# Decode attention beside a SwiGLU feed-forward: how w_down, the end of V and the end of wo are loaded

## The chip, the cores and the metric

The kernel runs on one core of one Trainium2 chip. The metric is the device time of one execution in microseconds (us). One execution was also recorded by the hardware profiler; its trace gives the start and duration of every instruction and of every DMA packet. Engines: PE (matmuls; PEld its weight loads), DVE (vector), ACT (scalar), POOL (GpSimd), SP (here the issuer of nearly all DMAs). Sixteen DMA engines move the data of the core.

## The reference

One token is decoded by an attention block over a long cache and by a feed-forward block, and a scalar gate mixes the two. H is 32 heads, Sk 65,536 cached positions, Dh 128, D 512, F 1,792, all in bfloat16.

```
g = sigmoid((x * gate_w).sum(-1))
q = (x @ wq) in 32 heads of 128
p = softmax(q @ k_cache^T * 128**-0.5)         # 32 x 65536
a = (p @ v_cache) as 4096 values @ wo          # wo: 4096 x 512
b = (silu(x @ w_gate) * (x @ w_up)) @ w_down   # w_down: 1792 x 512
out = g * a + (1 - g) * b                      # 512 values
```

K and V have 536.9 MB each and are read once; everything else together is some 15 MB.

## The kernel before

**Tiles.** Each head's K and V are cut into G = 4 tiles of 16,384 positions; a tile is 128 partitions x 128 positions x 128 values, 4 MB, and n = 4h + g numbers the tiles from 0 to N - 1 = 127. All K and V tiles, and for a while wq, gate and up, w_down and the last wo rows, live in five slots of 4 MB. take(name) hands out the slot that has been free the longest and give(name) returns one, so the order of takes and gives in the program settles which load waits for which reader.

**Queues.** The schedule is written by hand: each engine runs its instructions in program order. SP issues the loads in program order; a load waits in SP until the readers of its slot are done, and the loads behind it wait with it. ACT issues only xT and gwT, at the start. Each DMA reports its completion through one of eight semaphores in turn, and a DMA is issued only when the last user of its semaphore has landed.

**A K tile.** DVE multiplies by the head's query (L254) and folds the 128 products to 64 or 32 by additions (L258); PE sums the rest with identity matmuls into S_ps (scores, L267); DVE folds it (L281). Per head, row_max and exponentials give P_sb, the weights.

**A V tile.** PE multiplies 4 columns of P_sb with 4 positions of the tile at a time: 32 matmuls of 128 x 512 into O_ps (values, L322). After a head's fourth V tile, ACT copies O_ps to O_sb (L335), head_turn turns it into a column by small matmuls (oh_ps, L351), ACT scales it to oT (L358), and project multiplies it with the head's 128 rows of wo into the two halves of a_ps (L365). For the last V tile the last TURNED = 8 positions are left to head_turn (L343).

**The loop.** A step loads and works one K tile and one V tile, with the V tiles some steps behind. load_wo(g) loads the wo rows of four heads (512 KB, two buffers) at v = 16g + 2, for g from 0 to 3. At v = N - 1 load_late loads the rows of the last 16 heads into a slot, in pieces of 5, 5, 4 and 2 heads. Heads 0 to 15 are projected in the loop, heads 16 to 31 after the last head_turn. The third and second to last V tiles come in two pieces each, the last one in pieces that end at columns 32, 64, 96, 112, 120 and 128.

**The start-up.** K 0 to 2 and wq are loaded first, then gate, K 3 and up. W_down (wd_t) takes the slot of K tile 1 behind scores(1). It lies on 64 partitions with 28 rows of w_down each, and comes in eight DMAs of 8 partitions (firsts lists the first of each, the step is 4), six ahead of load_k(4) and two behind it. load_k(4) takes the slot of wq, which is free once all queries are made. feed_forward_out runs in the step of K tile 4: two identity matmuls and an ACT copy bring the hidden values hT from 128 partitions x 14 to 64 x 28, then 28 matmuls of 64 x 512 make b_ps (L233), ACT copies it (L236) and four matmuls start a_ps with it (L238). The slot of w_down then goes to K tile 6 by the order of the free list.

Of the kernel before, what the change touches and what calls it, by code (L numbers as in the profile page):

```python
# [8 lines left out]
ACT = mybir.ActivationFunctionType  # L9
ALU = mybir.AluOpType  # L10
AXIS = mybir.AxisListType
P = 128
# [3 lines left out]
NB = 128  # L16
# [7 lines left out]
SPREAD = 40  # L24

WG = 4
LATE = 16
LATE_CUTS = (0, 5, 10, 14, LATE)
TURNED = 8
V_CUTS = {3: (0, 64, NB), 2: (0, 64, NB), 1: (0, 32, 64, 96, 112, NB - TURNED, NB)}  # L30


@with_exitstack
def kernel(
# [14 lines left out]
    nc = tc.nc  # L49
    bf16 = mybir.dt.bfloat16  # L50
    f32 = mybir.dt.float32

    _, H, Sk, Dh = A_k_cache.shape
    D = A_x.shape[2]
    F = B_w_gate.shape[1]
    KT = D // P
    FT = F // P
    G = Sk // (NB * P)
# [6 lines left out]
    consts = ctx.enter_context(tc.tile_pool(name="consts", bufs=1))  # L65
# [7 lines left out]
    psum_m = ctx.enter_context(tc.tile_pool(name="psum_m", bufs=2, space=bass.MemoryType.PSUM))  # L73
# [7 lines left out]
    def take(name):  # L81
        slot = free.pop(0)
        held[name] = slot
        return ring.tile(
            [P, NB * Dh], bf16, name=name.split(".")[0], tag=f"slot{slot}"
        )

    def give(name):
        free.append(held.pop(name))
# [14 lines left out]
    def load(dst, cache, n, name, cuts=(0, NB), slot=None):  # L104
        h, g = divmod(n, G)
        t = take(f"{name}.{n}") if slot is None else slot
        view = t.rearrange("p (j d) -> p j d", d=Dh)
        src = cache[0, h, g * NB * P : (g + 1) * NB * P, :].rearrange("(p j) d -> p j d", j=NB)
        for a, b in zip(cuts[:-1], cuts[1:]):
            nc.sync.dma_start(out=view[:, a:b, :], in_=src[:, a:b, :])  # L110
        dst[n] = view

    def load_k(n):
        load(K_tiles, A_k_cache, n, "K_t")

    def load_v(n):
        load(V_tiles, A_v_cache, n, "V_t", V_CUTS.get(N - n, (0, NB)))

# [9 lines left out]
    ident_b = consts.tile([P, P], bf16, name="ident_b")  # L128
# [29 lines left out]
    wo_tiles = {}  # L158

    def load_wo(g):  # L160
        wo_tiles[g] = wo_pool.tile([P, WG, D], bf16, name="wo_sb", tag="wo_sb")
        rows = A_wo[g * WG * P : (g + 1) * WG * P, :]
        nc.sync.dma_start(out=wo_tiles[g], in_=rows.rearrange("(h p) n -> p h n", p=P))

    def load_late(cuts):
        late = take("wo_late.0")[:, : LATE * D].rearrange("p (h n) -> p h n", n=D)
        rows = A_wo[(H - LATE) * P :, :].rearrange("(h p) n -> p h n", p=P)
        for a, b in zip(cuts[:-1], cuts[1:]):
            nc.sync.dma_start(out=late[:, a:b, :], in_=rows[:, a:b, :])
        return late  # L170

    def feed_forward_in():
        gu_ps = psum_m.tile([P, 2 * FT], f32, name="gu_ps", tag="misc")
        for w in range(2):
            cols = wgu_sb[:, w].rearrange("p t (m c) -> p t c m", c=FT)
            for ft in range(FT):
                for t in range(KT):
                    nc.tensor.matmul(
                        gu_ps[:, w * FT + ft : w * FT + ft + 1],
                        lhsT=cols[:, t, ft, :],  # L180
                        rhs=xT[:, t : t + 1],
                        start=(t == 0),
                        stop=(t == KT - 1),
                    )
        gu_sb = consts.tile([P, 2 * FT], f32, name="gu_sb")
        nc.scalar.activation(out=gu_sb, in_=gu_ps, func=ACT.Copy)
        eg = consts.tile([P, FT], f32, name="eg")
        nc.scalar.activation(out=eg, in_=gu_sb[:, :FT], func=ACT.Exp, scale=-1.0)
        return gu_sb, eg
# [32 lines left out]

    def feed_forward_out(hT, rest):
        b_ps = psum_m.tile([1, D], f32, name="b_ps", tag="misc")
        h_ps = psum_m.tile([HP, GT], f32, name="h_ps", tag="misc")
        for r in range(2):
            nc.tensor.matmul(
                h_ps[:, r * FT : (r + 1) * FT], lhsT=ident_b[:, r::2], rhs=hT, start=True, stop=True
            )
        h2 = consts.tile([HP, GT], bf16, name="h2")  # L230
        nc.scalar.activation(out=h2, in_=h_ps, func=ACT.Copy)  # L231
        for t in range(GT):
            nc.tensor.matmul(  # L233
                b_ps, lhsT=h2[:, t : t + 1], rhs=wd_sb[:, t, :], start=(t == 0), stop=(t == GT - 1)
            )
        nc.scalar.activation(out=b_sb, in_=b_ps, func=ACT.Copy, scale=rest)  # L236
        for i, a in enumerate(a_ps):
            nc.tensor.matmul(  # L238
                a, lhsT=ones_f[0:1, 0:1], rhs=b_sb[:, i * HD : (i + 1) * HD], start=True, stop=False
            )  # L240
# [22 lines left out]
    def scores(n):  # L263
        S = F_tiles[n] = psum_s.tile([P, NB, QUAD], f32, name="S_ps")
        width = width_of(n)
        for c in range(0, width, QUAD):
            nc.tensor.matmul(  # L267
                S,
                lhsT=ident_b,
                rhs=K_tiles[n][:, :, c : c + QUAD],  # L270
                start=(c == 0),
                stop=(c == width - QUAD),
            )
        del K_tiles[n]
        give(f"K_t.{n}")
# [84 lines left out]
        )  # L360

    def project(h):
        rows = wo_tiles[h // WG][:, h % WG, :] if h < H - LATE else wo_late[:, h - (H - LATE), :]
        for i, a in enumerate(a_ps):
            nc.tensor.matmul(  # L365
                a,
                lhsT=oT[:, h : h + 1],
                rhs=rows[:, i * HD : (i + 1) * HD],
                start=False,
                stop=(h == H - 1),  # L370
            )


    def score_tile(n):
        for _ in products(n):
            pass
        if n:
            fold(n - 1)
# [11 lines left out]
    score_tile(1)  # L390
    xs = gate_sum()
    scores(1)
    wd_t = take("wd_t.0")
    HP = P // 2
    GT = F // HP
    wd_sb = wd_t[:HP, : GT * D].rearrange("p (t n) -> p t n", t=GT)
    wd_rows = B_w_down.rearrange("(p t) n -> p t n", t=GT)
    firsts = (0, 1, 2, 3, 32, 33, 34, 35)

    def load_wd(i):  # L400
        part = slice(firsts[i], firsts[i] + 29, 4)
        nc.sync.dma_start(out=wd_sb[part], in_=wd_rows[part])

    for i in range(6):
        load_wd(i)
    for g in range(1, H // QG):
        queries(g)
    give("wq_t.0")
    eg2 = gate_exp(xs)
    load_k(4)  # L410
    load_wd(6)
    load_wd(7)
    score_tile(2)
    rest = gate_value(eg2)
    scores(2)
# [7 lines left out]
    v = 0  # L423
# [5 lines left out]
        steps.append((None, v))  # L429
        v += 1  # L430

    done = tot_ps = wo_late = None
    for n, v in steps:
        if n is not None and n > G:
            load_k(n)
        if v is not None:
            if v % (WG * G) == 2 and v // (WG * G) < (H - LATE) // WG:
                load_wo(v // (WG * G))
            if v:
                load_v(v)  # L440
            if v == N - 1:
                wo_late = load_late(LATE_CUTS)
        vector = iter(()) if n is None else products(n)
        top_of = None
        if n is None:
            top_of = H - 1 if F_tiles else None
        elif n % G == 0:
            top_of = n // G - 1
            vector = (i for a in (0, NB // 2) for i in products(n, a, a + NB // 2))
        if top_of is not None:  # L450
            next(vector, None)
            fold(top_of * G + G - 1)
            mT_ps = row_max(top_of)
            next(vector, None)
            exponentials(top_of, mT_ps)
        if n == G:
            hT = feed_forward_mid(*ff)
        for _ in vector:
            pass
        if n is not None and n % G:  # L460
            fold(n - 1)
        if tot_ps is not None:
            weight(*tot_ps)
            tot_ps = None
        if n == G:
            feed_forward_out(hT, rest)
            give("wd_t.0")
        if done is not None:
            head_turn(done, head_copy(done))
        if v is not None:  # L470
            values(v)
        if top_of is not None:
            tot_ps = top_of, total(top_of)
        if n is not None:
            scores(n)
        if done is not None and done < H - LATE:
            project(done)
        done = v // G if v is not None and v % G == G - 1 else None
    head_turn(H - 1, head_copy(H - 1))
    for h in range(H - LATE, H):  # L480
        project(h)

    out_sb = consts.tile([1, D], bf16, name="out_sb")
# [33 lines left out]
```

## Time and profile before

| What | Value |
|---|---|
| Median of 3 runs | 2534.09 us (2533.99 to 2534.16) |
| Profiled execution | 2534.41 us, of which the span of its instructions is 2532.6 us |
| DMA traffic | 1088.49 MB, mean 430 GB/s over the span |
| DVE busy | 2083.7 us (82%) |
| PE busy | 1533.7 us (61%), mean granted clock 0.772 |
| ACT busy | 77.7 us (3%) |
| K tile, issue to landing | 35.3 us (median) |
| V tile, issue to landing | 28.0 us (median) |

The profile names a group of instructions by engine, line and tiles (out<-in). A line of a timeline has start, duration, engine, line and operation, the number of instructions, and in brackets the engine's idle time before it with what ended that idle time. The chain of waits has start, duration and what it was; it runs back from the last instruction to whatever released each step. A table of windows has, for each stretch, its length, the busy time of PE, PEld, DVE, ACT and POOL with the number of instructions, the granted clock of PE, the mean busy share of the 16 DMA engines, and GB/s. A line of waits has who waited, for whom, the time in total, how often, and the longest one.

### The profile page before, as it was taken

To read this page: it belongs to the slowest core of one execution; us is meant where nothing else is said; L and a number is where in the kernel's file an instruction comes from. 1 tells how busy PE (TensorE), PEld (TensorE's weight loads), DVE (VectorE), ACT (ScalarE), POOL (GpSimd) and SP (SyncE) were. 2 spreads that over 40 slices of the span, in tenths; PEclk is the share of its full clock that TensorE was granted. 3 is DMA by queue.
4 is the path that set the end of the run, shared out by engine and by line. 5 is a ranking of instruction groups with operands and counts; after the bars stand their busy time and mean duration, and the time that the engine had idled before them with its cause. 6 is when DMAs were issued, how large, how long until landed. Compare 5 with 4: busy or idle time off the path is not lost.

```text
span 2532.6 us, 13195 instructions
## 1 busy us (share of the span) xinstructions
PE 1533.7 (61%) x5786; PEld 581.6 (23%) x5786; DVE 2083.7 (82%) x744; ACT 77.7 (3%) x208; POOL 0.9 (0%) x7
## 2 busy tenths in 40 slices
PE   4656656665566555555665566556656665665569
PEld 1222222222222112222222122222222221222223
DVE  7788888888887999988888888888888888888860
ACT  1000000000000000000000000000000000000000
POOL 0000000000000000000000000000000000000000
PEclk9777777777777787787777777777777777777779
DMA  9999999999999999999999999999999999999998
GB/s 412 418 431 433 435 432 430 434 433 432 431 433 434 431 433 434 432 431 434 433 432 433 434 432 432 435 431 432 432 434 432 431 435 433 431 434 433 432 432 351
DMA packets 43915, 1088.49 MB, mean 430 GB/s; under 512 B 4753, under 2 KB 9362, under 8 KB 10258
## 3 DMA queue, kind: packets, MB, share of 16 engines
q1 hardware_dynamic: 43570, 1087.65, 99.7%
q8 instruction: 45, 0.74, 0.1%
q14 instruction: 12, 0.10, 0.0%
q10 hardware_dynamic: 288, 0.00, 0.0%
HBM read 1087.64 MB, written 0.00 MB: 429 GB/s over the span
## 4 chain that ended last, share of the span: by engine, by line
DMA 71%; PE 23%; DVE 4%; issue 1%; ACT 0%; SPq 0%; DVEq 0%
DMA V_t<-in_A_v_cache_dram 63%; PE O_ps L322 21%; DMA K_t<-in_A_k_cache_dram 8%; DVE K_t L254 3%; DVE K_t L258 1%; PE S_ps L267 1%; DMA wo_late<-in_A_wo_dram 0%; PE b_ps L233 0%; DVE S_sb L281 0%; DVE m L287 0%; PE oh_ps L351 0%; PE a_ps L238 0%; ACT P_sb L300 0%; PE a_ps L365 0%; PE mT_ps L291 0%
## 5 line engine op out<-in xcount | busy, mean ns | idle before, releaser
L322 PE MATMUL O_ps<-V_t,P_sb 128*4 128x512 bf16 x4094 | 1154.5, 452 | 663.5 <-DMA V_t<-in_A_v_cache_dram 663.5
L254 DVE TENSOR_TENSOR K_t<-K_t,q_bc 128x16384 bf16<-128x16384 bf16 (+1 forms) x159 | 1117.2, 7026 | 357.9 <-DMA K_t<-in_A_k_cache_dram 346.7
L258 DVE TENSOR_TENSOR K_t<-K_t 128x8192 bf16<-128x8192 bf16 (+1 forms) x314 | 859.7, 2738 | 8.6
L322 PEld LDWEIGHTS <-P_sb 128*4 128x4 bf16 x4094 | 393.0, 97 | 1405.1 <-issue 1064.1
L267 PE MATMUL S_ps<-K_t,ident_b 128*128 128x512 bf16 x1056 | 263.3, 393 | 100.6 <-DVE K_t L258 100.6
L267 PEld LDWEIGHTS <-ident_b 128*128 128x128 bf16 x1056 | 98.0, 101 | 248.0 <-issue 158.0
L291 PE MATMUL mT_ps<-diag,ones_f 128*128 128x128 f32 x64 | 24.5, 483 | 150.1 <-ACT diag L289 150.1
L351 PE MATMUL oh_ps<-ident_f,O_sb 4*128 4x1 f32 x256 | 55.5, 334 | 74.5 <-ACT O_sb L335 74.5
L281 DVE TENSOR_REDUCE S_sb<-S_ps 128x128 f32<-128x512 f32 x128 | 87.5, 683 | 4.9 <-PE S_ps L267 4.9
L289 ACT ACTIVATE diag<-ident_f,m 128x128 f32<-128x128 f32 x32 | 12.8, 401 | 2118.7 <-DVE m L287 2118.7
L351 PEld LDWEIGHTS oh_ps<-ident_f,O_sb 4*128 4x128 f32 x256 | 52.8, 301 | 84.1 <-ACT O_sb L335 82.9
L291 PEld LDWEIGHTS mT_ps<-diag,ones_f 128*128 128x128 f32 x64 | 15.2, 295 | 166.7 <-ACT diag L289 166.7
L484 DVE CAST out_sb<-a_ps 1x256 bf16<-1x256 f32 x1 | 0.4, 412 | 56.6 <-PE a_ps L365 56.6
L300 ACT ACTIVATE P_sb<-S_sb,bias 128x512 bf16<-128x512 f32 x32 | 23.1, 722 | 1.0
L287 DVE TENSOR_REDUCE m<-S_sb 128x1 f32<-128x512 f32 x32 | 22.0, 686 | 1.1
L335 ACT ACTIVATE O_sb<-O_ps 4x512 f32<-4x512 f32 x32 | 18.3, 572 | 129.2 <-PE O_ps L322 129.2
L313 DVE RECIPROCAL recip<-tot_ps 128x1 f32<-128x1 f32 x32 | 5.1, 158 | 13.0 <-PE tot_ps L308 13.0
L308 PEld LDWEIGHTS tot_ps<-rowsum,ones_f 128*128 128x128 f32 x64 | 9.5, 188 | 14.0 <-issue 14.0
L233 PE MATMUL b_ps<-wd_t,h 64*1 64x512 bf16 x28 | 12.1, 625 | 0.3 <-ACT h L231 0.3
L308 PE MATMUL tot_ps<-rowsum,ones_f 128*128 128x1 f32 x64 | 12.2, 260 | 0.0
L358 ACT ACTIVATE oT<-oh_ps,rg 128x1 bf16<-128x1 f32 x32 | 8.4, 263 | 65.0 <-PE oh_ps L351 65.0
L296 DVE TENSOR_REDUCE top<-mT_ps 128x1 f32<-128x128 f32 x32 | 9.1, 284 | 1.0 <-PE mT_ps L291 1.0
(47 smaller groups left out, 75.2 us busy)
## 6 DMA issues: line engine op xcount, KB each, us to landing
K_t<-in_A_k_cache_dram SPq DMA_DIRECT2D x128, 4096.0 KB, 35.3
V_t<-in_A_v_cache_dram SPq DMA_DIRECT2D x125, 4096.0 KB, 28.0
V_t<-in_A_v_cache_dram SPq DMA_DIRECT2D x4, 2048.0 KB, 31.1
wq_t<-in_A_wq_dram SPq DMA_DIRECT2D x1, 3584.0 KB
V_t<-in_A_v_cache_dram SPq DMA_DIRECT2D x3, 1024.0 KB
wo_sb<-in_A_wo_dram SPq DMA_DIRECT2D x4, 512.0 KB, 38.8
gu_t<-in_B_w_gate_dram SPq DMA_DIRECT2D x1, 1792.0 KB
gu_t<-in_B_w_up_dram SPq DMA_DIRECT2D x1, 1792.0 KB
```

Of the source, the lines that this page charges most:

```text
L254: yield nc.vector.tensor_tensor(out=K, in0=K, in1=q_rep, op=ALU.mult)
L258: yield nc.vector.tensor_tensor(out=K[:, :, 0:half], in0=K[:, :, 0:half], in1=K[:, :, half : 2 * half], op=ALU.add,)
L267: nc.tensor.matmul(S, lhsT=ident_b, rhs=K_tiles[n][:, :, c : c + QUAD], start=(c == 0), stop=(c == width - QUAD),)
L281: nc.vector.tensor_reduce(out=S_tiles[h][:, g * NB : (g + 1) * NB], in_=F_tiles.pop(n), axis=AXIS.X, op=ALU.add)
L287: nc.vector.tensor_reduce(out=m, in_=S_tiles[h], axis=AXIS.X, op=ALU.max)
L289: nc.scalar.activation(out=diag, in_=ident_f, func=ACT.Copy, scale=m)
L291: nc.tensor.matmul(mT_ps, lhsT=ones_f, rhs=diag, start=True, stop=True)
L300: nc.scalar.activation(out=P_tiles[h], in_=S_tiles[h], func=ACT.Exp, bias=bias, scale=scale, accum_out=rowsum[:, h : h + 1],)
L308: nc.tensor.matmul(tot_ps, lhsT=ones_f, rhs=rowsum[:, h : h + 1], start=True, stop=True)
L322: nc.tensor.matmul(O_tiles[h], lhsT=P_tiles[h][:, g * NB + j : g * NB + j + 4], rhs=V_tiles[n][:, j : j + 4, :], start=(g == 0 and j == 0) ...
L335: nc.scalar.activation(out=O_sb, in_=O_tiles.pop(h), func=ACT.Copy)
L351: nc.tensor.matmul(oh_ps, lhsT=O_sb[:, c * Dh : (c + 1) * Dh], rhs=ident_f[0:4, c : c + 1], start=(c == 0 and not turned), stop=(c == 3),)
```

## The change

W_down lies on all 128 partitions with 14 rows each, and is one DMA of 1,792 KB. The Activation engine issues it, behind the queries' copies and the gate's exponential in its program; it takes the slot that wq gave back. K tile 4 is loaded ahead of it in the program and takes the slot of K tile 1. feed_forward_out multiplies hT directly: 14 matmuls of 128 x 512 take the place of the two identity matmuls, the ACT copy and 28 matmuls. The wo rows of all heads are loaded four heads at a time into the two wo buffers, the last four heads' rows behind the last V tile, and only heads 28 to 31 are projected after the last head_turn. The pieces of the last V tile that ended at columns 112 and 120 become one.

```diff
-LATE = 16
-LATE_CUTS = (0, 5, 10, 14, LATE)
 TURNED = 8
-V_CUTS = {3: (0, 64, NB), 2: (0, 64, NB), 1: (0, 32, 64, 96, 112, NB - TURNED, NB)}
+V_CUTS = {3: (0, 64, NB), 2: (0, 64, NB), 1: (0, 32, 64, 96, NB - TURNED, NB)}
...
-    def load_late(cuts):
-        late = take("wo_late.0")[:, : LATE * D].rearrange("p (h n) -> p h n", n=D)
-        rows = A_wo[(H - LATE) * P :, :].rearrange("(h p) n -> p h n", p=P)
-        for a, b in zip(cuts[:-1], cuts[1:]):
-            nc.sync.dma_start(out=late[:, a:b, :], in_=rows[:, a:b, :])
-        return late
...
         b_ps = psum_m.tile([1, D], f32, name="b_ps", tag="misc")
-        h_ps = psum_m.tile([HP, GT], f32, name="h_ps", tag="misc")
-        for r in range(2):
-            nc.tensor.matmul(
-                h_ps[:, r * FT : (r + 1) * FT], lhsT=ident_b[:, r::2], rhs=hT, start=True, stop=True
-            )
-        h2 = consts.tile([HP, GT], bf16, name="h2")
-        nc.scalar.activation(out=h2, in_=h_ps, func=ACT.Copy)
-        for t in range(GT):
-            nc.tensor.matmul(
-                b_ps, lhsT=h2[:, t : t + 1], rhs=wd_sb[:, t, :], start=(t == 0), stop=(t == GT - 1)
+        for t in range(FT):
+            nc.tensor.matmul(
+                b_ps, lhsT=hT[:, t : t + 1], rhs=wd_sb[:, t, :], start=(t == 0), stop=(t == FT - 1)
             )
...
-        rows = wo_tiles[h // WG][:, h % WG, :] if h < H - LATE else wo_late[:, h - (H - LATE), :]
+        rows = wo_tiles[h // WG][:, h % WG, :]
...
     scores(1)
-    wd_t = take("wd_t.0")
-    HP = P // 2
-    GT = F // HP
-    wd_sb = wd_t[:HP, : GT * D].rearrange("p (t n) -> p t n", t=GT)
-    wd_rows = B_w_down.rearrange("(p t) n -> p t n", t=GT)
-    firsts = (0, 1, 2, 3, 32, 33, 34, 35)
-
-    def load_wd(i):
-        part = slice(firsts[i], firsts[i] + 29, 4)
-        nc.sync.dma_start(out=wd_sb[part], in_=wd_rows[part])
-
-    for i in range(6):
-        load_wd(i)
     for g in range(1, H // QG):
         queries(g)
     give("wq_t.0")
     eg2 = gate_exp(xs)
     load_k(4)
-    load_wd(6)
-    load_wd(7)
+    wd_t = take("wd_t.0")
+    wd_sb = wd_t[:, : FT * D].rearrange("p (t n) -> p t n", t=FT)
+    nc.scalar.dma_start(out=wd_sb, in_=B_w_down.rearrange("(p t) n -> p t n", t=FT))
     score_tile(2)
...
-            if v % (WG * G) == 2 and v // (WG * G) < (H - LATE) // WG:
+            if v % (WG * G) == 2 and v // (WG * G) < H // WG - 1:
                 load_wo(v // (WG * G))
             if v:
                 load_v(v)
             if v == N - 1:
-                wo_late = load_late(LATE_CUTS)
+                load_wo(H // WG - 1)
...
-        if done is not None and done < H - LATE:
+        if done is not None and done < H - WG:
             project(done)
         done = v // G if v is not None and v % G == G - 1 else None
     head_turn(H - 1, head_copy(H - 1))
-    for h in range(H - LATE, H):
+    for h in range(H - WG, H):
         project(h)
```

More of the change, by code (lines that the diff above doesn't have):

```diff
@@ L430 @@
         v += 1
-    done = tot_ps = wo_late = None
+    done = tot_ps = None
     for n, v in steps:
```

## The prediction

> **What bounds the kernel now.** I read the page first: DMA by slices, the queues, the chain.
>
> ```profile
> DMA  9999999999999999999999999999999999999998
> GB/s 412 418 431 433 435 432 430 434 433 432 431 433 434 431 433 434 432 431 434 433 432 433 434 432 432 435 431 432 432 434 432 431 435 433 431 434 433 432 432 351
> q1 hardware_dynamic: 43570, 1087.65, 99.7%
> DMA 71%; PE 23%; DVE 4%; issue 1%; ACT 0%; SPq 0%; DVEq 0%
> ```
>
> The 16 DMA engines are busy for nearly the whole span. The change leaves the bytes alone, so only three things can move the time: how evenly the bytes lie on the sixteen engines, whether an engine ever runs out of queued work, and what follows the last transfers. The last slice (351 GB/s against 430) asks for the tail: the chain of waits there, then a table of windows.
>
> ```profile
> 2486.99 29.42 DMA V_t<-in_A_v_cache_dram
> 2516.42 12.18 DMA wo_late<-in_A_wo_dram
> 2528.65 1.48 PE a_ps L365 x12
> ...
> 2530.15 0.37 ACT out_sb L485
> ```
> ```profile
> 2514.00:2516.00 2.00, 2.00 (x10) 0.81 (x10) 0.00 (x0) 0.00 (x0) 0.00 (x0) 1.00 0.92 357
> ...
> 2520.00:2522.00 2.00, 1.72 (x9) 0.59 (x8) 0.00 (x0) 0.00 (x0) 0.00 (x0) 1.00 0.38 137
> ...
> 2526.00:2528.00 2.00, 2.00 (x20) 1.58 (x21) 0.00 (x0) 0.26 (x1) 0.00 (x0) 1.00 0.11 39
> 2528.00:2530.00 2.00, 1.95 (x18) 1.25 (x15) 0.00 (x0) 0.00 (x0) 0.00 (x0) 1.00 0.03 11
> ```
>
> The chain ends on wo_late, yet the last two columns of the windows (DMA share, GB/s) fade over 15 us. One engine moves some 27 GB/s (430/16), so 39 GB/s is one or two engines: most are done and wait for the slowest. The end is that engine's end.
>
> Which one it is, I took from the trace's records of single DMA packets. On a busy engine a packet starts 3 or 4 ns before the one ahead of it ends, so the records string into sixteen chains. A 32,768 B packet takes 1.213 us, a 28,672 B one 1.062, a 14,336 B one 0.535, a 1,024 B one 0.046. W_down's 28,672 B rows are 64 packets, all on the same eight engines: with 8 partitions, a DMA uses 8 engines. So eight engines carry 8 x 1.062 = 8.5 us of w_down and the other eight nothing. The V piece of columns 96 to 112 ends between 2513.5 and 2522.2 us on the eight with w_down, between 2508.3 and 2517.0 on the others. Within each set the fastest and slowest differ by 8.7 us; this comes from the instruction-queue packets, each of which costs its engine 1.4 us and which fall on some engines only. From 2527.3 to 2528.93 one engine alone runs, one with w_down, a 1 KB packet every 42 ns; it had work without a break to there.
>
> By the Trainium skill (DMA: Bandwidth & Descriptors, section "Why a DMA increments its semaphore by 16 and not by 1") a DMA runs on the largest number up to 16 that divides both patterns' slowest dimensions, from the lowest engines up. By that, 8 partitions are always the same 8 engines and 128 are 16; the trace agrees (4,465 completion records = 275 x 16 + 8 x 8 + 1).
>
> **The change, part by part.**
>
> *W_down over 16 engines.* 8 packets of 14,336 B on each, 8 x 0.535 = 4.3 us. The eight that had it lose 8.5 - 4.3 = 4.2 us, the other eight gain 4.3. The slowest engine of the run is of the first kind: -4.2. The second kind's slowest goes from 2517.0 to 2521.3 at that V piece, the first's from 2522.2 to 2518.0, so the second would lead with -0.9, unless it gets time back elsewhere. It does, in the start-up:
>
> ```profile
> SPq L110 <- PE b_ps L233: 19.5, 1, 19.5
> ```
> ```profile
> 87.97 12.10 PE L233 MATMUL b_ps<-wd_t,h 64*1 64x512 bf16 x28 [0.28 <-ACT h L231]
> ...
> 100.10 0.33 SPq L110 DMA_DIRECT2D K_t<-in_A_k_cache_dram  x1
> 100.48 0.43 SPq L163 DMA_DIRECT2D wo_sb<-in_A_wo_dram  x1
> ```
> ```profile
> 96.00:100.00 4.00, 4.00 (x10) 0.98 (x8) 0.52 (x2) 0.00 (x0) 0.00 (x0) 0.50 0.78 336
> ```
>
> K tile 6 takes w_down's slot and is issued only when the 28 matmuls are done, at 100.10. The eight engines without w_down end everything queued at 99.3 to 100.8 us: the DMA share dips to 0.78. They end K tile 6 12.6 us after V tile 1, where 9.68 (8 x 1.209) is usual: 2.8 us lost. The other eight, 8.5 us behind, lose 0.3.
>
> After the change K tile 4 takes K tile 1's slot (free at 46.4, when the first w_down piece was issued) and no longer waits for the queries (57.01). W_down is issued by ACT behind the last q_bc copy, at 53.0, into wq's slot. Both then stand in the engines' queues, ahead of V tile 0. All sixteen engines, free of the up weights at 60.4, do K 4 and w_down to 74.4, V 0 to 84.0, K 5 to 93.7, V 1 to 103.4. DVE took K 4 at 78.44 and should at about 75; hT (87.4) comes at about 84; 14 matmuls instead of 28 at 12.10/28 = 0.43 us are 6.0 us, the two ident_b matmuls and the ACT copy (0.29 and 0.20) are gone, so K 6 is issued at about 90, 13 us before any engine is dry. That is the 2.8 us of the second set: 2521.3 becomes 2518.5, level with the first. Hence -4.2 for the DMA stream, -0.9 if that cover fails.
>
> *ACT as issuer.* Not in the trace in this place; xT's issue on ACT took 0.38 us and landed in 1.8. ACT is idle from 53.1 to 66.84 behind it, so its issue costs nothing; what waits for ACT next is gu_sb at 66.84. Its packets may share the engines with K 3's end and the up weights, whose landing can slip by up to 4.3 us: the gate and up matmuls end at 68 instead of 66.8, which holds up K 5's issue by that much, 16 us before it is needed. SP issues the 8 pieces no more (4.19 us for the first six, 1.71 for two), and nothing behind them on SP waits for them.
>
> *Wo of heads 16 to 27 in the loop.* Three more loads of 512 KB, at 32 packets of 0.0424 = 1.36 us an engine, 4.1 us in all, now lie ahead of the last V tile instead of behind it: no bytes more. 12 heads x 2 matmuls of 0.27 us move into the loop, where PE is 61% busy and waits for V: nothing (bound: 24 x 0.27 = 6.5 us if PE had no idle time, and it has 39%).
>
> *The tail.* The timeline of before:
>
> ```profile
> 2521.35 3.18 PE L322 MATMUL O_ps<-V_t,P_sb 128*4 128x512 bf16 x14 [0.28 <-DMA V_t<-in_A_v_cache_dram]
> ...
> 2524.63 0.59 ACT L335 ACTIVATE O_sb<-O_ps 4x512 f32<-4x512 f32 x1 [28.74 <-PE O_ps L322]
> ...
> 2526.25 3.87 PE L365 MATMUL a_ps<-wo_late,oT 128*1 128x256 bf16 x32
> ...
> 2530.55 0.29 SPq L486 DMA_DIRECT2D out_dram<-out_sb  x1
> ```
>
> On the slowest engine V columns 64 to 96 end at 2520.95. After: -4.2 + 4.1 = 2520.85; columns 96 to 120, one piece, 1.89 us later at 2522.74 (PE sees a landing 0.4 us after its last record: 2523.15); 120 to 128 at 2523.4, wo at 2524.75. PE: columns 64 to 96 are 8 matmuls of 0.22 to 2523.0, then 6 of 0.22 to 2524.5; O_sb as before at 2524.6; the rest runs as before to oT at 2526.6. Six projections fit under oT, two follow, to 2527.2; out_sb 0.4; out DMA at 2527.6 instead of 2530.55. So the tail gives back 1.2 of the 4.2: before, wo covered the last head's turn, now 0.5 MB can't. Larger pieces cost PE nothing else: its wait moves to columns 96 to 120.
>
> Fewer DMAs also lift a limit: in the tail each DMA is issued only when the eighth before it has landed (wo's last at 2521.46), so fast engines ran dry. After, all are queued by about 2500. This helps fast engines only: no gain at the end.
>
> Sum: -4.2 + 1.2 = -3.0 us. The profiled execution took 2534.41 (span 2532.6 and 1.8 around it), so 2531.4; on the median of 2534.09, **2531.1**.
>
> **Rivals.**
>
> *No time back (13%).* The second set still runs dry: -0.9 + 1.2 = +0.3, 2534.4. For it: w_down reaches its engines late. Against: K 6 has 13 us in hand.
>
> *Slower (8%, and 3% for what I don't see).* The engines serve SP's queue first, so w_down comes behind V 1, and lands at 103.4. Then b_ps ends at about 110, K 6 is issued behind it, its first packets come 1.8 us later, and all engines stand idle for some 8 us: -3.0 + 8 = +5, 2539.2. It decides from a landing of w_down later than about 95 us (8 us of matmuls and issue before 103.4), and each us beyond costs one. Against: xT, from ACT, landed in 1.8 us. No DMA of ACT beside a loaded SP queue is in this trace. The Trainium skill (DMA: Bandwidth & Descriptors, section "Issuing engines are not separate DMA queues") says that transfers of different issuers run on the same 16 DMA engines and interleave; by that w_down comes early.
>
> *Faster (12%).* The slowest engine gets one instruction packet less (-1.4), and an earlier V piece hides the tail's 1.2: -4.2 - 1.4 = -5.6, 2528.5. These packets move with the instruction count; 45 fall on some eight engines, five or six each.
>
> *Each DMA has a fixed cost (2%).* Eight DMAs fewer (w_down 7, V 1; wo has eight in both), each worth what a small one takes to land (1.8 us for xT): 2534 - 14 = 2520. Against: between two DMAs of one engine lies only a completion record, some 6 ns, and the next data packet follows at once. The Trainium skill (DMA: Bandwidth & Descriptors, section "Anatomy of one DMA", a fit for DMAs issued by GpSimd) gives about 2.0 us plus bytes by 436 GB/s for each DMA; by that 16 us would go. Queued back to back as here, the trace shows none of it.
>
> **How the numbers follow.** 62% for 2531.1, whose own errors (the level of the two sets, 1.4 us for one instruction packet) are about 1.5 us each way. With the first rival the range runs from 2528.6 to 2535.0; left out are the slower cases, the fixed cost and part of the faster one. 0.2% is 5.1 us, about what a measurement of this kernel can tell from no change: faster 12 + 2 = 14%, slower 11%, within 75%.
>
> **What would show it.** Right: no DMA dip at 96 to 100, K 6's issue near 90, b_ps x14 of some 6 us, SP's wait for b_ps down from 19.5 to some 13; the windows of the last 15 us falling later and steeper; PE's last wait on V, not on wo; out DMA near 2527.6. Wrong: a dip before 130 us with w_down as releaser, a tail in which one or two engines still run alone for 2 us or more, or K and V tiles that land slower in the loop beside the three wo loads.

## The result: slower by 7.7 us, and the profile after

| | Median | Against before |
|---|---|---|
| Before | 2534.09 us (2532.63 to 2534.2) | |
| Changed kernel | 2541.77 us (2541.53 to 2541.88) | 1.0031, 95% interval 1.0021 to 1.0041 |

The times of the kernel before lie at two levels, near 2532.6 and near 2534.2, and its median is of the upper one. The prediction said 2531.1, with 2528.6 to 2535.0 as its range. The profiled execution's span went from 2532.6 to 2539.8 us.

First the start-up, where the change was to show. The wait of SP, PE's b_ps in the timeline, SP's issues, and the window from 96 to 100 us of the changed kernel:

```profile
SPq L108 <- PE b_ps L217: 13.3, 1, 13.3
```
```profile
85.54 4.66 PE L217 MATMUL b_ps<-wd_t,hT 128*1 128x512 bf16 x14 [1.94 <-DVE hT L211]
...
90.22 0.33 SPq L108 DMA_DIRECT2D K_t<-in_A_k_cache_dram  x1
90.60 0.43 SPq L161 DMA_DIRECT2D wo_sb<-in_A_wo_dram  x1
```
```profile
96.00:100.00 4.00, 4.00 (x20) 1.65 (x19) 3.69 (x1) 0.00 (x0) 0.00 (x0) 1.00 0.95 410
```

This is what was forecast: K tile 6 is issued at 90.22 (90 said), SP's wait is 13.3 us (13 said), and the dip to a DMA share of 0.78 is gone. Nothing is lost here. Now the end, in the chain of waits, the windows and the timeline:

```profile
2497.67 33.46 DMA V_t<-in_A_v_cache_dram
2531.13 0.04 issue
2531.17 3.35 PE O_ps L306 x14
```
```profile
2526.00:2528.00 2.00, 2.00 (x11) 0.77 (x9) 0.00 (x0) 0.00 (x0) 0.00 (x0) 1.00 0.63 257
...
2532.00:2534.00 2.00, 2.00 (x10) 0.76 (x9) 0.00 (x0) 0.00 (x0) 0.00 (x0) 1.00 0.44 160
2534.00:2536.00 2.00, 1.55 (x18) 1.02 (x15) 0.00 (x0) 0.59 (x1) 0.00 (x0) 1.00 0.08 26
```
```profile
2534.61 0.59 ACT L319 ACTIVATE O_sb<-O_ps 4x512 f32<-4x512 f32 x1 [28.89 <-PE O_ps L306]
...
2537.69 0.33 SPq L458 DMA_DIRECT2D out_dram<-out_sb  x1
```

The last wait is for V, as said; the DMA share in the windows falls later and more steeply than before; and from O_sb to the out DMA it takes 3.1 us (3.0 said). But all of it lies 10 us late: O_sb at 2534.6 where 2524.6 was worked out. The time went before the tail. Rate of the DMA engines by slices, from the page:

```profile
GB/s 408 430 434 431 429 432 429 431 433 431 431 430 431 432 431 431 432 429 432 431 430 432 429 433 430 431 432 429 432 430 431 432 432 429 431 432 431 431 431 359
```

Before, most slices lay between 431 and 435; here most lie between 429 and 432, evenly over the whole run. The view of the DMA queues for 500 to 2400 us, where neither start nor end takes part, says the same; first before, then the changed kernel:

```profile
DMA packets 29266, 822.22 MB, mean 433 GB/s; under 512 B 3159, under 2 KB 4183, under 8 KB 4183
```
```profile
DMA packets 30682, 818.83 MB, mean 431 GB/s; under 512 B 3191, under 2 KB 5751, under 8 KB 5751
```

Less data in the same time, though the engines' queue packets take 100.2% of it in both. So the packets themselves are longer. The packet records of the two traces: of 32,384 packets of 32,768 B (one row of a K or V tile each), 32,200 took 1.213 us before. After, only 2,197 do; from 130 to 2400 us 28% take 1.220 to 1.226, most of the rest 1.214 to 1.219, and the mean there is 1.2179 against 1.2138. An engine without instruction packets takes 9.714 us for a tile where 9.681 was usual: over the 256 tiles that is 8.5 us. The changed kernel's packets are clean at first (91% at 1.213 between 45 and 60 us) and longer from about 60 us on, for good.

### The profile page after: what moved, and what is told of

Its sections match the earlier page's. It is cut to its first block, busy times and chain, and to the rows that moved or that the text cites. A ratio compares the mean times of both kernels' runs of the same rounds, so it can differ in the third digit from the quotient of the medians.

```text
span 2539.8 us, 13146 instructions
## 1 busy us (share of the span) xinstructions
PE 1529.1 (60%) x5770; PEld 579.5 (23%) x5770; DVE 2083.8 (82%) x744; ACT 77.5 (3%) x207; POOL 0.9 (0%) x7
## 4 chain that ended last, share of the span: by engine, by line
DMA 72%; PE 22%; DVE 5%; issue 0%; ACT 0%; SPq 0%; DVEq 0%; ACTq 0%
DMA V_t<-in_A_v_cache_dram 65%; PE O_ps L306 21%; DMA K_t<-in_A_k_cache_dram 7%; DVE K_t L238 3%; DVE K_t L242 2%; PE S_ps L251 1%; DVE S_sb L265 0%; PE oh_ps L335 0%; DVE m L271 0%; ACT P_sb L284 0%; ACT O_sb L319 0%; PE mT_ps L275 0%; PE a_ps L349 0%; DVE top L280 0%; ACT diag L273 0%
## 5 line engine op out<-in xcount | busy, mean ns | idle before, releaser
L349 PE MATMUL a_ps<-wo_sb,oT 128*1 128x256 bf16 x64 | 11.7, 271 | 0.0
```

## The experiments

Three theories were set against each other: the queue that issued w_down (Q), the phase of the engines among themselves, which w_down on eight of them had kept apart (P), and the pieces of the end (T). Below, "packets of 1.213" are runs in which over 99% of the 32,768 B packets take 1.213 us; "packets of 1.218" gives the mean from 130 to 2400 us where most are longer.

**The issuer alone.** W_down's one DMA by SP.

```diff
-    nc.scalar.dma_start(out=wd_sb, in_=B_w_down.rearrange("(p t) n -> p t n", t=FT))
+    nc.sync.dma_start(out=wd_sb, in_=B_w_down.rearrange("(p t) n -> p t n", t=FT))
```

> The changed kernel, with w_down's one DMA issued by SP instead of ACT, at the same place of the program. Theory Q (the queue): a transfer through ACT's queue leaves every later packet of the run longer (32,768 B packets 1.213 us before, 1.218 on average after); without it the packets are back at 1.213 and the balance of the prediction shows, 2531 us. Theory P (the phase): before, eight engines run half a tile behind the other eight because of w_down, and the change puts all sixteen in step, where they disturb each other; then it stays at 2541 to 2542 with packets of 1.218. Theory T (the tail) says 2541 to 2542 too, with packets of 1.213.

Measured: 2541.54 us (1.0030, interval 1.0019 to 1.0041), packets of 1.218. Q falls: the issuer makes no difference.

**The end alone.** The kernel before with the change's V pieces, wo loads and last projections.

> The kernel before with only the end changed: V pieces ending at 96, 120, 128, wo in loads of four heads, heads 28 to 31 projected at the end; w_down as before. Theories Q and P both give packets of 1.213 us and the price of the tail alone, 2534.1 + 1.2 = 2535.3. Theory T, by which the end's pieces are what costs, gives 2540 or more.

Measured: 2535.41 us, packets of 1.213. The end costs 1.3 us by the medians (1.0005, interval 0.9996 to 1.0014, so it isn't clear of nothing on that measure). T falls.

**W_down alone.** The changed kernel with the end as before.

> The kernel before with only w_down changed: one DMA on 128 partitions issued by ACT, 14 matmuls, K tile 4 in the slot of K tile 1; the end as before. Theories Q and P both give packets of 1.218 us and 2541.8 less the tail's 1.2, 2540.6. Theory T gives 2531 to 2534.

Measured: 2540.18 us (1.0025, interval 1.0015 to 1.0035), packets of 1.218. This part of the change alone costs 6 us.

**Eight DMAs by ACT.** The kernel before with `nc.scalar` for `nc.sync` in load_wd.

> The kernel before with its eight w_down DMAs, of 8 partitions each, issued by ACT instead of SP; nothing else. Theory Q: packets of 1.218 us from w_down on, 2534.1 + 8.6 = 2542.7 or so. Theory P: the eight engines still run half a tile behind, packets of 1.213, 2534. If the queue spoils only the engines that it used, those eight alone have longer packets, and the time is that of the slowest of them, again 2542.

Measured: 2534.11 us (1.0000), packets of 1.213. Q falls a second time. P was still open, and what else the w_down part holds: K tile 4's slot, 128 partitions, and one tile fewer. That last was the lead. The change drops h2, 56 bytes a partition, and the pools lie one behind the other, so all that comes behind h2 moves 64 bytes down. The five slots start at byte 30,976 of each partition before (121 x 256) and at 30,912 after (120 x 256 + 192). Theory A: the address.

**Sixty-four bytes back.**

```diff
+    pad = consts.tile([P, 32], bf16, name="pad")
     xT = consts.tile([P, KT], bf16, name="xT")
```

> The changed kernel with one unused tile of 64 bytes a partition put ahead of the others, nothing else. In the kernel before the five slots start at byte 30,976 of a partition, a multiple of 256; the change drops the tile h2 (56 bytes), and they start at 30,912, which is 64 below such a multiple. Theory A (the address): each packet into a slot that starts off a multiple of 256 is longer; with the pad the slots are at 30,976 again, packets at 1.213 us, and the time is that of the prediction's sum, 2531. Theory P (the phase of the engines, w_down on 16 of them): unchanged, 2541 to 2542 with packets of 1.217 to 1.218.

Measured: 2531.48 us (0.9990, interval 0.9981 to 0.9999). The whole change, with an unused tile, is 10.3 us faster than the change without it. Of its 32,768 B packets 32,276 take 1.213 us. The queue view from 500 to 2400 us, and the end of the timeline:

```profile
DMA packets 30789, 821.83 MB, mean 433 GB/s; under 512 B 3206, under 2 KB 5766, under 8 KB 5766
```
```profile
2520.90 3.30 PE L307 MATMUL O_ps<-V_t,P_sb 128*4 128x512 bf16 x14 [0.26 <-DMA V_t<-in_A_v_cache_dram]
...
2524.29 0.59 ACT L320 ACTIVATE O_sb<-O_ps 4x512 f32<-4x512 f32 x1 [30.47 <-PE O_ps L307]
...
2527.38 0.33 SPq L459 DMA_DIRECT2D out_dram<-out_sb  x1
```

The rate is 433 again, O_sb starts at 2524.3 and the out DMA goes at 2527.4.

**The kernel before, shifted.** `[P, 96]` in place of `[P, 32]`, in the kernel before: slots at 31,168 = 121 x 256 + 192.

> The kernel before with an unused tile of 192 bytes a partition ahead of the others: the slots start at 31,168, 64 bytes below a multiple of 256 as in the changed kernel; w_down, the end and all else as before. Theory A: packets of 1.217 us, 2534.1 + 8.6 = 2542 to 2543. Theory P: 2534 with packets of 1.213.

Measured: 2544.44 us (1.0041, interval 1.0028 to 1.0053), packets of 1.218. Nothing but addresses differs from the kernel before, and that costs 10.3 us. P can't explain this: the eight engines with w_down are the same as before. The queue view from 500 to 2400 us:

```profile
DMA packets 29171, 819.22 MB, mean 431 GB/s; under 512 B 3156, under 2 KB 4180, under 8 KB 4180
```

**All of w_down on eight engines, slots off.**

```diff
+    wd_rows = B_w_down.rearrange("(p t) n -> p t n", t=FT)
+    for a in range(0, P, 8):
+        nc.sync.dma_start(out=wd_sb[a : a + 8], in_=wd_rows[a : a + 8])
```

> The changed kernel (slots at 30,912) with w_down's 128 partitions loaded by sixteen DMAs of 8 partitions, issued by SP: all of w_down on eight engines again, 16 x 0.535 = 8.6 us on each. Theory P: the eight run half a tile behind, packets of 1.213, 2534.1 and the tail's 1.3, 2535.4. Theory A: packets of 1.217, and the eight engines' 4.3 us on top of the changed kernel's time, 2545 to 2546.

Measured: 2563.99 us (five runs from 2552.91 to 2567.35), packets of 1.218 from 200 us on. By the packets P falls here too, but the time is 18 us over what A expected, so the time says nothing of either. The timeline of SP and the windows show where it went:

```profile
53.58 31.38 SPq L386 DMA_DIRECT2D wd_t<-in_B_w_down_dram  x16
86.33 0.36 SPq L108 DMA_DIRECT2D V_t<-in_A_v_cache_dram  x1
```
```profile
60.00:80.00 20.00, 11.05 (x108) 7.34 (x106) 14.52 (x4) 0.41 (x2) 0.00 (x0) 0.74 0.79 256
80.00:100.00 20.00, 0.79 (x2) 0.50 (x2) 14.02 (x13) 1.42 (x4) 0.00 (x0) 0.52 0.83 111
```

With eight semaphores each of the sixteen DMAs waits for the eighth before it, SP is held for 31 us, V tile 0 goes out at 86 instead of 60, and the rate falls to 256 and 111 GB/s: 20 x (1 - 256/434) + 20 x (1 - 111/434) = 23 us of transfers missing. 2541.8 + 23 is the time of the profiled execution, 2564.8. The pieces were slow themselves, too: from 71 to 97 us their 14,336 B rows took 1.56 to 2.13 us each by the packet records, where 0.535 was usual. Each of these DMAs writes eight partitions in a row; those of before wrote eight that lie four apart, and their 28,672 B rows took 1.062. The experiment thus changed more than the number of engines, and whether the neighbouring partitions made the rows slow was not tried apart.

**W_down of the change, the end of before, and the pad.**

> W_down as in the changed kernel, the end as before, and the 64 byte pad. Theory A: 2534.1 - 4.2 to - 5.0 (w_down on 16 engines, the end's 1.3 not paid) = 2529 to 2530, faster than both kernels. Theory P: 2540, as without the pad (2540.2).

Measured: 2529.82 us (0.9985, interval 0.9976 to 0.9994), the fastest so far, 4.3 us under before. Against the version without the pad (2540.18) the 64 bytes are 10.4 us.

**Which multiple.** The same kernel with pads of 192, 128, 320 and 32 bytes.

> The fastest kernel so far (w_down as in the change, the end as before, 2529.82 us with slots at 30,976) with a pad of 192 bytes in place of 64: slots at 31,104, 128 above a multiple of 256. If what counts is a multiple of 256 (theory A256), packets are 1.217 and the time is 2540; if a multiple of 128 is enough (A128), 1.213 and 2530.

Measured: 2539.87 us, packets of 1.218. A multiple of 128 isn't enough.

> The same with a pad of 128 bytes: slots at 31,040, 64 above a multiple of 256. A256 and A128 both give 1.217 and 2540; if only the distance of 192 that the change made is bad, 2530.

Measured: 2540.09 us, packets of 1.218: the change's own distance is not the only bad one.

> The same with a pad of 320 bytes: slots at 31,232, a multiple of 512; 30,976 is one of 256 only. A256: 1.213 and 2529.8, no difference. If 512 counted, packets would be shorter than 1.213 and the time below 2529.

Measured: 2529.79 us, packets of 1.213: a multiple of 512 gains nothing over one of 256.

> The same with a pad of 32 bytes: slots at 30,944, 32 below a multiple of 256 and a multiple of 32 only. A256: 1.217 and 2540 as at 64 below; if the price grows with a finer misfit, longer packets and over 2541.

Measured: 2542.45 us (1.0033, interval 1.0020 to 1.0046), packets of 1.2188, hardly one of them at 1.213, and longer already at 45 us. Off by 32 costs 2.4 us more than off by 64.

So 256 is the step: three distances of 64, 128 and 192 all cost 10 us, a distance of 0 or 256 in 512 nothing. In all these runs every later tile moves with the slots, the wo buffers too, and their 1,024 B packets also got longer: 0.0489 us on average in the changed kernel, 0.0460 with the pad. So did the instruction packets of queue q8, from 0.93 us in the runs at a multiple of 256 to 1.07 in those off it. That the slots' own address makes the 32,768 B packets longer is therefore argued, from the packets that go into them, and was not tried apart from the other tiles' addresses.

## Why the prediction was wrong

The step that failed is its opening: "The change leaves the bytes alone, so only three things can move the time: how evenly the bytes lie on the sixteen engines, whether an engine ever runs out of queued work, and what follows the last transfers." There is a fourth: how long one packet takes, which the sum carried over from before (1.213 us) without a reason. The part on b_ps counted the two matmuls and the copy that go with h2, 0.29 and 0.20 us, and not that h2 was also 64 bytes of address below every slot. That term is +10.3 us (2541.77 - 2531.48), against a sum of -3.0. By the packet records some 8.5 of it are the tiles. The seven wo loads of the loop add about 0.6 on each engine (32 packets a load, 2.9 ns each), and the instruction packets 0.7 to 0.8 on an engine that carries five or six of them, if each holds it up by the 0.14 us that it got longer. The last 0.4 us or so were not followed.

None of the rivals had this mechanism. "Slower" had w_down land behind V 1; the changed kernel's b_ps started at 85.5 us, so w_down was there by then. The 3% for what was not seen is where the result fell.

With the address put back, the prediction's own sum can be checked term by term:

- *W_down over 16 engines, -4.2.* The pad with the old end gives 2529.82 - 2534.1 = -4.3, against the upper of the two levels of before; against the lower, 2532.6, it is -2.8. So the size is right to about the 1.5 us that the prediction gave itself, and the closer agreement is in part luck. The 2.8 us that the second set of engines was to get back came back: K 6's issue and the missing dip are shown above, and with the pad the V piece that ends at column 120 reaches the engines over 8.9 us, about the 8.7 within each set before.
- *The tail, +1.2.* 1.7 between the two padded kernels (2531.48 - 2529.82); without the pad 1.3 on the kernel before and 1.6 on the changed one (2541.77 - 2540.18): right, a little small.
- *The sum, 2531.1.* 2531.48 with the pad.
- *ACT as issuer, nothing.* 2541.54 by SP, 2541.77 by ACT: right. The up weights came later than said, though: PE waits 3.50 us for them in the changed kernel and the gate and up matmuls end at 70.4, not 68. K 5 was issued at 70.40 for it, which cost nothing.
- *DVE at K 4 at about 75.* 76.56. *b_ps 6.0 us.* 4.66: the granted clock was 0.67 there and 0.50 in the b_ps stretch of before, whose time per matmul the prediction took over.
- *Wo in the loop, nothing.* With the pad the rate from 500 to 2400 us is 433 GB/s with the three loads in it: right.
- *Fixed cost per DMA.* Eight DMAs fewer gave nothing of 14 us: right.

## What to carry to other kernels

In a kernel that the DMA engines bound, the address at which the big tiles start is part of the tuning: work out that address from all that lies ahead of them, and bring it back to a multiple of 256, by an unused tile if need be, whenever a small tile comes or goes. Here one line of 64 bytes was worth 10.3 us. When a time moves the other way than a sum that the start-up and the tail bear out, compare the length of single packets, not only what waits for them. And a forecast of a change should list the tiles that it adds and drops with the addresses that follow, as it lists instructions.

## What the runs showed of the hardware

A 32,768 B packet into a slot that starts off a multiple of 256 bytes takes 1.2179 us on average where 1.2138 was the average before, 0.3%, and 1.2188 where it is off a multiple of 64 as well. The price goes by the packet and hardly by its bytes: 4.1 ns on 32,768 B, 3.6 on w_down's 14,336 B (0.5393 us with the pad, 0.5429 without), 2.9 on wo's 1,024 B, which is 6% of those. The Trainium skill (DMA: Bandwidth & Descriptors, section "How a descriptor splits into AXI transactions") says that transactions are of 256 B and start at multiples of 256, so that a descriptor that starts off one needs one more. By that count 129 for 128 would be 0.8%, an estimate; the runs here give 0.3%, and they moved the address in SBUF that is written, where the page speaks of bytes fetched. The step of 256 agrees.

Packet by packet the price is no fixed amount: a few ns on most 32,768 B packets of the changed kernel, 7 to 13 ns on 28% of them. And they were not there from the start: between 45 and 60 us, nine in ten packets into the same slots still took 1.213. Why the price sets in only then is open, and so is why the instruction packets share in it.

As one DMA on 128 partitions, w_down is 144 packets in ACT's queue (432 against 288 before): 128 rows and 16 completion records, so all sixteen engines. An unequal load early on is not evened out later: before, of the 8.5 us that eight engines had more than the others at 80 us, and of which the dry stretch took some 3, 5.2 us were left between the fastest of the two sets at 2.5 ms.
